# A softmax guard as a reduction with a constant column, the first half's sums of x moved into attention, and one clamp moved to ScalarE

## The chip, the cores and the metric

The kernel runs on one core of a Trainium2 chip. The metric is the device time of one execution in microseconds, taken as the median of several runs. The engines are named as in the profile: PE is TensorE (matmuls; PEld its weight loads), DVE is VectorE, ACT is ScalarE, POOL is GpSimd, and SP is the engine whose queue issues the DMAs.

## The reference

Three layers follow each other. The shapes are batch 2, 8 heads, sequence 576, head size 64, so 1152 tokens with 512 features; the mixture has 4 experts of width 1024, the last layer has width 1536. Everything is float32.

```python
# attention with a decay from the clamped, cumulated gates s
cum = np.cumsum(np.maximum(s, 0.0), axis=-1)
bias = -(cum[:, :, :, None] - cum[:, :, None, :])
scores = np.where(causal, -1e9, scale * q @ k.T + np.minimum(bias, 0.0))
attn = np.exp(scores - scores.max(-1, keepdims=True))
attn = attn / (attn.sum(-1, keepdims=True) + 1e-09)
x = attn @ v                                   # 1152 x 512
# a dense mixture of 4 experts
p = domain_probs / (domain_probs.sum(-1, keepdims=True) + 1e-09)
x = sum(p[:, e:e+1] * (np.maximum(x @ w1[e], 0.0) @ w2[e]) for e in range(4))
# a gated layer
g = x @ w_gate
out = (g / (1 + np.exp(-g)) * (x @ w_val)) @ w_out
```

## The kernel before

**Precision.** Dense products are made from three matmuls in a reduced format: each operand is held as a high part and a low part (`xh`, `xl` for x, `wah`, `wal` for an input weight, `woh`, `wol` for an output weight, `hh`, `hl` for the hidden layer), and high times high, high times low and low times high are added up in PSUM. Making a high part is a cast (helper `move`, L325 on ACT, L327 on DVE, L329 on POOL), making a low part is a subtraction (helper `minus`, L338, on DVE or POOL).

**Attention.** The sequence is cut into an early part (positions 0 to 255) and a late part (256 to 575). There are 16 pairs of heads: eight early ones and then eight late ones. For each pair PE makes the scores (`sp`, L528 to L547); DVE adds bias and mask and takes the row's minimum of the negated scores (`least`, L562, written to a small statistics tile `st`); ACT takes the exponential and its row sum (L571, to columns 8 to 11 of `st`); DVE adds 1e-9 to two row sums at a time and takes the reciprocal (`guard`, L577 and L578, 40 times in all); ACT or POOL scales the rows (`norm`, L333 or L335); PE transposes them (`tp`, L622); ACT or DVE copies the result (`p`, L325 or L327); PE multiplies with v (`po`, L681); ACT or DVE and then DVE write `xh` and `xl` (L697). The late part's decay comes from a scan over the clamped gates: `positive` (L394), `scan` (L397), `center` (L402, tile `sums`), a small store to memory (`rows`), from which each late pair's bias is loaded by DMA (`dql`, `d`; the latter gets a mask added, L493).

**Dense work.** Hidden units go in slices of 256 (a slice is an input weight and an output weight of 512 KB each). As soon as the first early x is done, input products (L1016 to L1018) and output products (L1177 to L1179) for the first 256 or 512 tokens are put between the attention steps on PE. Until the end of attention POOL alone makes the high and low parts of the weights (L329, L338). Each output product is scaled by its expert's share and added to an accumulator on DVE (`acc_a`, `acc_b`, L1275).

**The sums of x.** After attention, input products are made in a form with seven instead of eight block products (`seven`, L1116 to L1118). For it four sums of quarters of x are needed for the first 512 tokens and again for the other 640 (`sums_of_x`). One call makes, for two column blocks each, nine additions or subtractions into a temporary `tt` (18 instructions, L1055), eight casts (L325) and eight low parts (L338), that is 34 instructions of 128 x 256 elements for the first 512 tokens and of 128 x 320 for the rest. Before the change both calls stand behind the end of attention, when their tiles `xh0`, `xl0`, `xh512`, `xl512` are made; additions and low parts go to DVE or POOL, casts to ACT or DVE.

**What sets the order.** Nothing is scheduled at run time. A planner in the file (`Plan`) holds all tasks with estimated costs, their dependences, the buffers they take and a rank. It emits again and again the task that can start first by its own clock of each engine, and among equals the one of lowest rank. `any_of` lets it choose the engine too. What it emits is each engine's instruction order, so an instruction that has to wait holds up everything behind it on its engine. The planner has a clock of its own for the port that it takes DVE and POOL to share, but `guard` and `positive` do not count on it.

Of the kernel before, what the change touches and what calls it, by code (L numbers as in the profile page):

```python
# [1 line left out]

# [6 lines left out]
F32 = mybir.dt.float32  # L9
F32R = mybir.dt.float32r  # L10
I32 = mybir.dt.int32
U32 = mybir.dt.uint32
AF = mybir.ActivationFunctionType
ALU = mybir.AluOpType
# [89 lines left out]
def act(c, n=1):  # L104
    return n * 0.05 + 0.00084 * c
# [173 lines left out]
def attention_moe_swiglu(ctx, tc, q_early, q_late, k, v, s, dp, w1, w2, wg, wv, wo, out):  # L279
# [37 lines left out]
    def ring(name, n=2):  # L317
        return rings.setdefault(name, Ring(n))

    def any_of(engines, kind, c, run, deps, n=1, **kw):  # L320
        return add(choices(engines, kind, c, n), None, run, deps, port="vp" if kind in ("two", "copy", "scale") else "p", **kw)
# [27 lines left out]
    def attention(ap, ps):  # L349
# [43 lines left out]
        def positive(e, x):  # L393
            {"v": nc.vector, "p": nc.gpsimd}[e].tensor_scalar(sr[:, x], sr[:, x], 0.0, -1.0 / SC, op0=ALU.max, op1=ALU.mult)  # L394
# [15 lines left out]
            sb, ncum[:, early], ncum[:, P - 1:P], 1.0, op0=ALU.subtract, op1=ALU.mult), [t_scan], rank=-98)]  # L410
        for j in range(2):
            t_early.append(add("dve", 0.41, lambda j=j: rest(j), t_early[-1:], rank=-98))
        t = any_of("v", "fill", S - 2 * P, lambda e: positive(e, later), [t_sr2], rank=CUM2)
        t.at = CUMAT
        t_scan2 = add("dve", 0.95, lambda: scan(later), [t, t_scan], rank=CUM2)

# [6 lines left out]
        if FILLER:  # L423
            def begin():
                plan.filler = keep_on
                plan.clock["pe"] = 1.65
            t_id.note = begin

        raw, t_raw, loaded = {}, {}, {}

# [76 lines left out]
        def group(i, pi, ch, qbs):  # L507
# [42 lines left out]
            def least(x, lane, at, w):  # L550
                def run():
                    if "st" not in box:
                        box["st"] = ap.tile([P, 20], F32, name="st", tag="st", bufs=6)
                    if lane not in box["ns"]:
                        box["ns"][lane] = ap.tile([P, S], F32, name="ns", tag="ns", bufs=NS)
                    st, ns = box["st"][:, 2 * x:2 * x + 2], box["ns"][lane]
                    if two:
                        todo = [(s0, s1, y[:, :s1 - s0], decay[pi, 2][:, s0:s1]) for y, (s0, s1) in zip(box["sp"], spans)]
                    else:
                        todo = [(at, at + w, box["sp"][lane][:, at:at + w], mask[:, 2 * P - w:] if pi < EXACT else decay[pi][:, lane, :w])]  # L560
                    for y, (s0, s1, sp, bias) in enumerate(todo):
                        nc.vector.tensor_tensor_reduce(  # L562
                            ns[:, s0:s1], sp, bias, SC, st[:, 0:1] if y else 3.0e38, op0=ALU.add, op1=ALU.min, accum_out=st[:, y:y + 1])
                return run
# [9 lines left out]
            def guard(x, n):  # L574
                def run():
                    st = box["st"]
                    nc.vector.tensor_scalar(st[:, 12 + x:12 + x + n], st[:, 8 + x:8 + x + n], 1.0e-9, None, op0=ALU.add)  # L577
                    nc.vector.reciprocal(st[:, 16 + x:16 + x + n], st[:, 12 + x:12 + x + n])  # L578
                return run

            def norm(x, lane, at, w):
# [373 lines left out]
    def make_weights(need):  # L955

        stop = min(len(queue), queue.index(need) + AHEAD)
        while made["n"] < stop:
            queue[made["n"]].make(WRANK + made["n"])
            made["n"] += 1  # L960
# [68 lines left out]
            return make  # L1029
        return [item(c0) for c0 in range(0, NC, step)]  # L1030

    def sums_of_x(t0):

        n = (N - HALF if t0 else HALF) // 2
        box = late["T", t0]

        deps = needs_x(t0, t0 + 2 * n) + late.get("sums", [])
        done = box["done"] = {}

        def quarter(x, i, j, c):  # L1040
            return f32(x[:, 2 * i + c, t0 + j * n:t0 + j * n + n])
        tmp = {}
        rg = ring("tt")

        rank = WRANK + made["n"] - (0 if t0 else 2)
        SUB, ADD = ALU.subtract, ALU.add

        def total(name, x, y, op, deps, new=False):

            def task(c, at):  # L1050
                def run(on):
                    if new and c == 0:
                        tmp[name] = late["t"].tile([P, 6 * P], F32, name="tt", tag="tt", bufs=2)[:, :2 * n].rearrange("p (c n) -> p c n", c=2)
                    x_, y_ = (tmp[z][:, c] if isinstance(z, str) else quarter(*z, c) for z in (x, y))
                    {"v": nc.vector, "p": nc.gpsimd}[on].tensor_tensor(tmp[name][:, c], x_, y_, op=op)  # L1055
                return any_of(TADD, "two", n, run, at, take=[rg] if new and c == 0 else [], rank=rank)
            first = task(0, deps[0])
            return [first, task(1, deps[1] + ([first] if new else []))]

        def chain(*lists):  # L1060
            return [[x[c] for x in lists] for c in range(2)]

        def parts(i, name, t):
            done[i] = []
            for c in range(2):
                def high(on, c=c):
                    move(on, box["h"][:, i, c], tmp[name][:, c])

                def low(on, c=c):
                    minus(on, box["l"][:, i, c], tmp[name][:, c], box["h"][:, i, c])  # L1070
                hi = any_of(THIGH, "copy", n, high, [t[c]], rank=rank)
                done[i].append(any_of(TLOW, "two", n, low, [hi], rank=rank))
            return done[i]
        a1 = total("T1", (xh, 0, 1), (xh, 0, 0), SUB, [deps, deps], True)
        t = total("T1", "T1", (xl, 0, 1), ADD, chain(a1))
        t1 = total("T1", "T1", (xl, 0, 0), SUB, chain(t))
        a2 = total("T2", (xh, 1, 1), "T1", SUB, chain(t1), True)
        t2 = total("T2", "T2", (xl, 1, 1), ADD, chain(a2))
        u2 = parts(1, "T2", t2)
        u1 = parts(0, "T1", t1)  # L1080

        t = total("T1", "T2", (xh, 0, 0), SUB, chain(u1, t2))
        t3 = total("T1", "T1", (xl, 0, 0), SUB, chain(t))
        u3 = parts(2, "T1", t3)
        add(None, 0.0, None, u3, give=[(a1[0], rg)])
        t = total("T2", (xh, 1, 0), "T2", SUB, chain(u2, t3))
        u4 = parts(3, "T2", total("T2", "T2", (xl, 1, 0), ADD, chain(t)))
        add(None, 0.0, None, u4, give=[(a2[0], rg)])
        late["sums"] = [x for y in done.values() for x in y]
# [418 lines left out]
    def gates(ap):  # L1508
        dps = ap.tile([P, NT, E], F32, name="dps", bufs=1)
        got = [add("dma", (ISSUE, 0.06), lambda: nc.sync.dma_start(dps, dp), rank=GRANK)]  # L1510
        got[0].at = GATES

        def run():
            sm = const.tile([P, NT], F32, name="sm")
            nc.vector.reduce_sum(sm, dps, axis=AX.X)
            nc.vector.tensor_scalar(sm, sm, 1.0e-9, None, op0=ALU.add)
            nc.vector.reciprocal(sm, sm)
            nc.vector.tensor_tensor(pr, dps, sm.unsqueeze(2).to_broadcast([P, NT, E]), op=ALU.mult)
        return add("dve", 0.8, run, got, rank=10)
# [11 lines left out]
    with ExitStack() as st:  # L1531
        ps = st.enter_context(tc.tile_pool(name="psa", bufs=1, space=PSUM))
        late["hA"] = ctx.enter_context(tc.tile_pool(name="hA", bufs=2))
        ap = st.enter_context(tc.tile_pool(name="ap", bufs=2))
        for _ in attention(ap, ps):
            pass
        late["gates"] = gates(ap)
        make_weights(queue[0])
        while any(x.end is None for g in done_x for x in done_x[g]):
            if all(x.end is not None for x in done_x[0]):  # L1540
                feed()
            assert plan.step()
        while plan.step(lambda t: not getattr(t, "dense", False) and t.rank < 1000 and t.eng != "dma"):
            pass
    with ExitStack() as st:
        late["ps"] = st.enter_context(tc.tile_pool(name="psb", bufs=1, space=PSUM, reuse_waits="tile"))
        late["t"] = st.enter_context(tc.tile_pool(name="tm", bufs=2, reuse_waits="tile"))
        late["h"] = late["t"]
        late["acc"] = late["t"].tile([P, NT - HALF // P, DM], F32, name="acc_b", bufs=1)
        for t0, n in ((0, HALF), (HALF, N - HALF)):  # L1550
            late["T", t0] = {x: late["t"].tile([P, 4, 2, n // 2], F32R, name=f"x{x}{t0}", bufs=1) for x in "hl"}
            sums_of_x(t0)
        late["made_n"] = 0
        plan.held, plan.ported = HELD2, False
        rings["h"].n, rings["o"].n = 5, 3
        feed()
        while plan.step():
            feed()
# [70 lines left out]
```

## Time and profile before

| | us |
|---|---|
| median of 3 runs (lowest, highest) | 710.91 (709.16, 711.38) |
| profiled execution, device time | 710.5 |
| its span in the profile | 708.7 |
| attention: first instruction to last `xl` (L697) | about 0 to 126.7 |
| both calls of the sums of x (L1055, L338) | 127.7 to 163 |
| dense work alone, in the seven-product form where it can be | from there to 705 |

The profile counts an engine as busy from an instruction's start to its end. PE's matmuls are pipelined, so overlapping ones hide short gaps; the rows for PE that carry an idle time in brackets are stretches in which nothing was in flight. The engine's own rows then say what released it.

### The profile page before, as it was taken

To read this page: it belongs to the slowest core of one execution; us is meant where nothing else is said; L and a number is where in the kernel's file an instruction comes from. 1 tells how busy PE (TensorE), PEld (TensorE's weight loads), DVE (VectorE), ACT (ScalarE), POOL (GpSimd) and SP (SyncE) were. 2 spreads that over 40 slices of the span, in tenths; PEclk is the share of its full clock that TensorE was granted. 3 is DMA by queue.
4 is the path that set the end of the run, shared out by engine and by line. 5 is a ranking of instruction groups with operands and counts; after the bars stand their busy time and mean duration, and the time that the engine had idled before them with its cause. 6 is when DMAs were issued, how large, how long until landed. Compare 5 with 4: busy or idle time off the path is not lost.

```text
span 708.7 us, 11847 instructions
## 1 busy us (share of the span) xinstructions
PE 695.1 (98%) x4243; PEld 605.8 (85%) x4243; DVE 552.8 (78%) x1087; ACT 357.4 (50%) x760; POOL 455.5 (64%) x434
## 2 busy tenths in 40 slices
PE   8899999999999999999999999999999999999997
PEld 7676666777999899989988889998989999999996
DVE  7876656793488898999899998786876878777665
ACT  7688776335354646456546665456554323333110
POOL 2873333978545865667558677698998848484311
PEclk9999999999999999999999999999999999999999
DMA  6695650220242434435525555213012201000003
GB/s 197 207 316 174 193 155 1 60 90 31 90 149 93 175 120 162 152 120 191 194 90 192 194 179 178 74 41 105 6 60 83 68 30 61 31 31 1 1 1 133
DMA packets 30187, 78.45 MB, mean 111 GB/s; under 512 B 3488, under 2 KB 8096, under 8 KB 30128
## 3 DMA queue, kind: packets, MB, share of 16 engines
q1 hardware_dynamic: 29984, 77.56, 33.4%
q8 instruction: 33, 0.54, 0.3%
q14 instruction: 26, 0.21, 0.1%
q10 hardware_dynamic: 144, 0.13, 0.1%
HBM read 65.85 MB, written 11.83 MB: 110 GB/s over the span
## 4 chain that ended last, share of the span: by engine, by line
PE 87%; DVE 7%; ACT 2%; POOL 1%; issue 1%; DMA 0%; DVEq 0%; POOLq 0%; ACTq 0%
PE h L1116 12%; PE o L1177 12%; PE h L1118 12%; PE h L1117 12%; PE o L1178 12%; PE o L1179 12%; PE tp L622 3%; PE po L681 2%; DVE tt L1055 2%; PE sp L540 2%; PE h L1016 2%; PE h L1017 1%; PE h L1018 1%; ACT ns L571 1%; PE sp L528 1%
## 5 line engine op out<-in xcount | busy, mean ns | idle before, releaser
L1135 DVE TENSOR_TENSOR cc<-cc,h 128x320 f32<-128x320 f32 (+1 forms) x282 | 126.4, 454 | 53.6 <-PE h L1118 45.7
L1177 PE MATMUL o<-woh,hh 128*128 128x512 f32 x397 | 157.4, 397 | 2.6 <-DVE acc_a L1275 2.5
L1178 PE MATMUL o<-wol,hh 128*128 128x512 f32 x397 | 156.0, 393 | 0.0
L1179 PE MATMUL o<-woh,hl 128*128 128x512 f32 x397 | 155.0, 390 | 1.0 <-DVE hl L338 1.0
L338 POOL TENSOR_TENSOR wal<-raw,wah 128x512 fp32r<-128x512 f32 (+1 forms) x58 | 73.1, 1270 | 31.5 <-ACT wah L325 30.2
L1116 PE MATMUL h<-xh,wsh 128*128 128x320 f32 (+1 forms) x312 | 93.1, 298 | 0.1
L1118 PE MATMUL h<-xh,wsl 128*128 128x320 f32 (+1 forms) x312 | 92.8, 298 | 0.0
L1117 PE MATMUL h<-xl,wsh 128*128 128x320 f32 (+1 forms) x312 | 92.7, 297 | 0.0
L1179 PEld LDWEIGHTS o<-woh,hl 128*128 128x128 f32 x397 | 74.7, 188 | 17.9 <-DVE hl L338 1.4
L338 POOL TENSOR_TENSOR hl<-cc,hh 128x512 fp32r<-128x512 f32 (+1 forms) x29 | 43.6, 1504 | 70.0 <-ACT hh L1247 68.8
L1177 PEld LDWEIGHTS o<-woh,hh 128*128 128x128 f32 x397 | 74.7, 188 | 16.1 <-DVE acc_a L1275 3.4
L1178 PEld LDWEIGHTS o<-wol,hh 128*128 128x128 f32 x397 | 74.7, 188 | 10.7
L338 POOL TENSOR_TENSOR wol<-raw,woh 128x512 fp32r<-128x512 f32 x54 | 77.8, 1457 | 7.0 <-ACT woh L325 6.0
L1244 ACT ACTIVATE cc<-cc 128x640 f32<-128x640 f32 (+1 forms) x46 | 32.1, 697 | 88.8 <-DVE cc L1135 88.8
L1116 PE MATMUL h<-xh,wah 128*128 128x320 f32 (+1 forms) x234 | 69.7, 298 | 0.9 <-DVE cc L1135 0.9
L1118 PE MATMUL h<-xh,wal 128*128 128x320 f32 (+1 forms) x234 | 69.4, 297 | 0.0
L1117 PE MATMUL h<-xl,wah 128*128 128x320 f32 (+1 forms) x234 | 69.3, 296 | 0.0
L338 POOL TENSOR_TENSOR wsl<-sf,wsh 128x512 fp32r<-128x512 f32 x44 | 64.1, 1478 | 2.2 <-ACT wsh L325 2.2
L1275 DVE SCALAR_TENSOR_TENSOR acc_b<-o,pr,acc_b 128x512 f32<-128x512 f32 x75 | 55.5, 744 | 7.0 <-PE o L1179 6.8
L1116 PEld LDWEIGHTS h<-xh,wsh 128*128 128x128 f32 x312 | 58.9, 189 | 1.9 <-ACT cc L325 0.3
L1117 PEld LDWEIGHTS h<-xl,wsh 128*128 128x128 f32 x312 | 59.0, 189 | 1.4
L1118 PEld LDWEIGHTS h<-xh,wsl 128*128 128x128 f32 x312 | 59.0, 189 | 0.0
(149 smaller groups left out, 1644.7 us busy)
## 6 DMA issues: line engine op xcount, KB each, us to landing
raw<-in_w SPq DMA_DIRECT2D x42, 512.0 KB, 5.0
n<-hl SPq DMA_DIRECT2D x36, 256.0 KB, 2.3
raw<-n SPq DMA_DIRECT2D x18, 512.0 KB, 3.3
hh<-in_wg SPq DMA_DIRECT2D x12, 512.0 KB, 4.1
hh<-in_wv SPq DMA_DIRECT2D x12, 512.0 KB, 4.3
hh<-in_wo SPq DMA_DIRECT2D x12, 512.0 KB, 4.1
dql<-rows SPq DMA_DIRECT2D x8, 512.0 KB, 5.1
vr<-in_v SPq DMA_DIRECT2D x4, 640.0 KB, 3.9
```

The lines of the kernel that those rows point to most:

```text
L338: {"v": nc.vector, "p": nc.gpsimd}[e].tensor_tensor(to, x, f32(y), op=ALU.subtract)
L540: nc.tensor.matmul(sp[j][:, at:at + w], Q[half[j], x], K[half[j], :w], start=True, stop=False)
L622: nc.tensor.transpose(tp[:kn, x * P:x * P + P], box["ns"][lane][:, at + c * P:at + c * P + kn], ident)
L1116: nc.tensor.matmul(hp, wh, h, start=c == 0, stop=False)
L1117: nc.tensor.matmul(hp, wh, l, start=False, stop=False)
L1118: nc.tensor.matmul(hp, wl, h, start=False, stop=c == 1)
L1135: nc.vector.tensor_tensor(part(k), part(x), banks[i], op=ALU.add)
L1177: nc.tensor.matmul(op, hh[:, f, ts], wh[:, f, y], start=f == 0, stop=False, skip_group_check=check)
L1178: nc.tensor.matmul(op, hh[:, f, ts], wl[:, f, y], start=False, stop=False, skip_group_check=check)
L1179: nc.tensor.matmul(op, hl[:, f, ts], wh[:, f, y], start=False, stop=f == NF - 1, skip_group_check=check)
L1244: nc.scalar.activation(src()[:, o], src()[:, o], AF.Relu)
L1275: nc.vector.scalar_tensor_tensor(acc(t), bank_(), sc, acc(t), op0=ALU.mult, op1=ALU.add)
```

## The change

1. `guard`: instead of adding 1e-9 with `tensor_scalar`, DVE sums pairs with `reduce_sum`; the second member of each pair is a column of `st` that holds 1e-9 all the time. For this the six statistics tiles are made once, used in turn, and their columns 12 to 15 are filled by six small POOL memsets at the start.
2. The sums of x of the first 512 tokens are planned during attention, with their own tiles: additions and low parts on POOL alone, casts on ACT or DVE as before. Their rank (150) lies behind that of attention's own tasks and of the weights that are then due. The sums of the other 640 tokens stay where they were.
3. The later gates' positive part (128 x 320) is an ACT Relu with a scale, instead of a DVE `tensor_scalar` with max and multiply.

```diff
-        t = any_of("v", "fill", S - 2 * P, lambda e: positive(e, later), [t_sr2], rank=CUM2)
+        t = add("act", act(S - 2 * P) + 0.15, lambda: nc.scalar.activation(sr[:, later], sr[:, later], AF.Relu, scale=-1.0 / SC), [t_sr2], rank=CUM2)
...
+        stat = [ap.tile([P, 24], F32, name=f"st{i}", bufs=1) for i in range(6)]
+        stats = cycle(stat)
+        for x in stat:
+            add("pool", 0.1, lambda x=x: nc.gpsimd.memset(x[:, 12:16], 1.0e-9), [t_up], rank=-97)
...
-                        box["st"] = ap.tile([P, 20], F32, name="st", tag="st", bufs=6)
+                        box["st"] = next(stats)
...
-                    nc.vector.tensor_scalar(st[:, 12 + x:12 + x + n], st[:, 8 + x:8 + x + n], 1.0e-9, None, op0=ALU.add)
-                    nc.vector.reciprocal(st[:, 16 + x:16 + x + n], st[:, 12 + x:12 + x + n])
+                    nc.vector.reduce_sum(st[:, 20 + x:20 + x + n], st[:, 8:16].rearrange("p (y x) -> p x y", y=2)[:, x:x + n], axis=AX.X)
+                    nc.vector.reciprocal(st[:, 16 + x:16 + x + n], st[:, 20 + x:20 + x + n])
...
-    def sums_of_x(t0):
+    def sums_of_x(t0, pool=None, add_on=TADD, low_on=TLOW):
...
-        rg = ring("tt")
-        rank = WRANK + made["n"] - (0 if t0 else 2)
+        rg = ring("te" if pool else "tt")
+        rank = WRANK + (50 if pool else made["n"])
...
         late["gates"] = gates(ap)
+        late["T", 0] = {x: const.tile([P, 4, 2, HALF // 2], F32R, name=f"x{x}0") for x in "hl"}
+        sums_of_x(0, ap, "p", "p")
         make_weights(queue[0])
...
-        for t0, n in ((0, HALF), (HALF, N - HALF)):
-            late["T", t0] = {x: late["t"].tile([P, 4, 2, n // 2], F32R, name=f"x{x}{t0}", bufs=1) for x in "hl"}
-            sums_of_x(t0)
+        late["T", HALF] = {x: late["t"].tile([P, 4, 2, (N - HALF) // 2], F32R, name=f"x{x}{HALF}", bufs=1) for x in "hl"}
+        sums_of_x(HALF)
```

## Rows read from the trace of the kernel before

**Rows 1.** The page: busy time by engine, and the chain that ended last.
```profile
PE 695.1 (98%) x4243; PEld 605.8 (85%) x4243; DVE 552.8 (78%) x1087; ACT 357.4 (50%) x760; POOL 455.5 (64%) x434
...
PE 87%; DVE 7%; ACT 2%; POOL 1%; issue 1%; DMA 0%; DVEq 0%; POOLq 0%; ACTq 0%
```

**Rows 2.** Order of time, PE: start, duration, line, idle before, releaser.
```profile
24.43 0.87 PE L681 MATMUL po<-p,vr 128*64 128x256 f32 x8 [1.28 <-DVE xl L697]
25.99 0.70 PE L533 MATMUL sp<-k,qe 64*128 64x128 f32 x5 [0.28 <-DVE st L562]
28.78 1.09 PE L622 MATMUL tp<-ident,ns 128*128 128x128 f32 x3 [1.17 <-ACT ns L333]
...
146.99 0.50 PE L1177 MATMUL o<-woh,hh 128*128 128x512 f32 x1 [1.68 <-DVE acc_a L1275]
160.69 0.50 PE L1177 MATMUL o<-woh,hh 128*128 128x512 f32 x1 [0.87 <-DVE acc_a L1275]
```

**Rows 3.** Stretches: busy PE, PEld, DVE, ACT, POOL, granted clock, DMA share, GB/s.
```profile
28.00:29.00 1.00, 0.22 (x1) 0.18 (x1) 0.96 (x6) 0.67 (x2) 0.92 (x3) 0.75 0.98 364
29.00:30.00 1.00, 1.00 (x5) 0.82 (x5) 0.95 (x5) 1.00 (x6) 1.00 (x2) 0.50 0.97 300
...
31.00:32.00 1.00, 1.00 (x7) 1.00 (x6) 0.40 (x4) 0.36 (x1) 1.00 (x2) 0.55 0.72 135
```

**Rows 4.** Order of time, DVE, 20 to 30 us.
```profile
20.91 1.39 DVE L394 TENSOR_SCALAR sr<-sr 128x320 f32<-128x320 f32 x1
22.34 0.98 DVE L397 TENSOR_TENSOR_SCAN ncum<-one,ncum,sr 128x320 f32<-128x320 f32 x1
...
23.96 0.41 DVE L697 TENSOR_TENSOR xl<-po,xh 128x256 fp32r<-128x256 f32 x1
26.80 1.24 DVE L577 TENSOR_SCALAR st<-st 128x2 f32<-128x2 f32 x1 [0.87 <-ACT ns L571]
29.49 0.18 DVE L1515 TENSOR_REDUCE sm<-dps 128x9 f32<-128x36 f32 x1
```

**Rows 5.** Order of time, POOL, 20 to 30 us.
```profile
20.85 1.27 POOL L338 TENSOR_TENSOR wal<-raw,wah 128x512 fp32r<-128x512 f32 x1
...
26.74 1.27 POOL L338 TENSOR_TENSOR wol<-raw,woh 128x512 fp32r<-128x512 f32 x1
...
28.68 1.27 POOL L338 TENSOR_TENSOR wol<-raw,woh 128x512 fp32r<-128x512 f32 x1
```

**Rows 6.** The guard's two lines: ns min/median/max, first and last start.
```profile
L577 DVE TENSOR_SCALAR st<-st x40: 142/169/1236, 7.7 to 119.7; 128x2 f32<-128x2 f32 x32, 128x1 f32<-128x1 f32 x8
...
L578 DVE RECIPROCAL st<-st x40: 162/166/167, 7.9 to 119.9; 128x2 f32<-128x2 f32 x32, 128x1 f32<-128x1 f32 x8
```

**Rows 7.** The tile `tt`: ns min/median/max, first and last start.
```profile
L325 ACT CAST xh<-tt x36: 299/407/462, 130.3 to 506.7; 128x256 fp32r<-128x256 f32 x24, 128x320 fp32r<-128x320 f32 x8, 128x128 fp32r<-128x128 f32 x4
...
L1055 DVE TENSOR_TENSOR tt<-tt,xl x12: 409/773/1509, 128.6 to 160.6; 128x320 f32<-128x320 f32 x7, 128x256 f32<-128x256 f32 x5
```

**Rows 8.** Stretches, columns as in rows 3.
```profile
45.00:95.00 50.00, 49.70 (x353) 34.14 (x354) 33.49 (x114) 41.05 (x102) 22.27 (x29) 1.00 0.64 202
```

**Rows 9.** Order of time, DVE, at 45 and 52 us.
```profile
44.97 0.40 DVE L697 TENSOR_TENSOR xl<-po,xh 128x256 fp32r<-128x256 f32 x1
...
52.49 0.23 DVE L493 TENSOR_TENSOR d<-d,tri 128x64 f32<-128x64 f32 x1 [1.42 <-DMA d<-rows]
```

**Rows 10.** Groups, whole span: line, shapes, count, busy us, mean ns, idle before.
```profile
L1055 POOL TENSOR_TENSOR tt<-xh 128x256 f32<-128x256 f32 x2 | 1.4, 744 | 0.0
...
L1613 POOL MEMSET const-float32-1.0<- 128x1 f32 x1 | 0.1, 98 | 0.0
```

**Rows 11.** The scaling on POOL (L335) alone: length, busy, clock, DMA share, GB/s.
```profile
45.00:95.00 50.00, 5.21 (x8) 1.00 0.64 202
```

**Rows 12.** Order of time, DVE, 144 to 147 us.
```profile
144.29 1.98 DVE L1055 TENSOR_TENSOR tt<-xh 128x320 f32<-128x320 f32 x2
146.20 0.74 DVE L1275 SCALAR_TENSOR_TENSOR acc_a<-o,pr,acc_a 128x512 f32<-128x512 f32 x1
```

More of the change, by code (lines that the diff above doesn't have):

```diff
@@ L1 @@
 from contextlib import ExitStack
+from itertools import cycle
 import concourse.bass as bass
@@ L1052, in run @@
                     if new and c == 0:
-                        tmp[name] = late["t"].tile([P, 6 * P], F32, name="tt", tag="tt", bufs=2)[:, :2 * n].rearrange("p (c n) -> p c n", c=2)
+                        tmp[name] = (pool.tile([P, 2 * n], F32, name="te", tag="te", bufs=2) if pool else late["t"].tile(
+                            [P, 6 * P], F32, name="tt", tag="tt", bufs=2)[:, :2 * n]).rearrange("p (c n) -> p c n", c=2)
                     x_, y_ = (tmp[z][:, c] if isinstance(z, str) else quarter(*z, c) for z in (x, y))
                     {"v": nc.vector, "p": nc.gpsimd}[on].tensor_tensor(tmp[name][:, c], x_, y_, op=op)
-                return any_of(TADD, "two", n, run, at, take=[rg] if new and c == 0 else [], rank=rank)
+                return any_of(add_on, "two", n, run, at, take=[rg] if new and c == 0 else [], rank=rank)
             first = task(0, deps[0])
@@ L1071, in parts @@
                 hi = any_of(THIGH, "copy", n, high, [t[c]], rank=rank)
-                done[i].append(any_of(TLOW, "two", n, low, [hi], rank=rank))
+                done[i].append(any_of(low_on, "two", n, low, [hi], rank=rank))
             return done[i]
```

## The prediction

> **What bounds the kernel now.** I read the page first. PE is busy for 98% of the span and makes 87% of the chain that ended last [rows 1]: the time is PE's work plus the stretches in which PE stands still or runs at a lower clock. So I looked for PE's own waits, in order of time. Up to 180 us, apart from the start and short ones, there are two clusters [rows 2]. At 24 to 29 us PE stands for 1.28, 0.28 and 1.17 us, together 2.73 us, released by `xl`, by the statistics and by the scaling. At 147 and 161 us it stands for 1.68 and 0.87 us, together 2.55 us, both times for a DVE accumulation into `acc_a`. The stretches of one microsecond then show a cost behind the first cluster: the granted clock is 0.75 at 28 us, 0.50 from 29 us (the 1.2 GHz level instead of 2.4) and 0.55 at 31 us, after PE was busy for only 0.22 us of the one at 28 [rows 3]. At half clock three microseconds do about 1.55 us of work, so about 1.45 us more is lost there (0.50 + 0.50 + 0.45, the middle second being like the one before it). First cluster: 2.73 + 1.45 = 4.18 us.
>
> DVE's order tells why the first cluster stands. The later gates' clamp L394 takes 1.39 us [rows 4] and ends where a POOL subtraction that ran beside it ends (20.85 + 1.27 = 22.12, the clamp at 22.30) [rows 5]. The scan follows, 0.98 us, then the centring up to 23.96, and only then the `xl` for which PE waits [rows 4]. The guard at 26.80 takes 1.24 us [rows 4], and ends at 28.04, just behind a POOL subtraction that ends at 28.01 [rows 5]; it is what the scaling, and so PE's third wait, waited for. Over the kernel a guard's first half takes 142 to 1236 ns with a median of 169, while the reciprocal right behind it always takes 162 to 167 [rows 6]. So this instruction waits for POOL, and the reciprocal doesn't.
>
> **The change, part by part.**
>
> *Guard.* The reduction reads four elements per row and writes two. The nearest row is the reduction over 128x36 at 29.49 us: 0.18 us, although it ran within a POOL subtraction (28.68 to 29.95) [rows 4, 5]. I take 0.17 us, as for an unhindered guard; bounds 0.14 and 0.18, which over 40 guards is -1.2 to +0.4 us of DVE time, none of it on PE's path unless PE waits. The guard's excess over 0.17 us goes: 1.07 us at 26.80.
>
> The Trainium skill ("VectorE: DVE Perf Modes", section "Rules for kernel authors") warns that a `tensor_reduce` on the hot path is the slowest DVE operation and should be restructured. The trace does not bear that out at this size (0.18 us beside POOL [rows 4]). By that rule the guards would get dearer; by the row they lose their wait.
>
> *Clamp.* 1.39 us leave DVE. On ACT the nearest row is a cast of 128x320 or less from SBUF, at most 462 ns [rows 7]; I take 0.46 us, bounds 0.30 (the least of that row) and 0.92 (with one more such cast ahead of it). ACT is not PE's releaser around 20 us. If it comes late, the scan stands on DVE, and behind it the `xl` that PE waits for; then up to the whole 1.28 us stays.
>
> *Gain in the first cluster.* With 1.39 us off DVE ahead of `xl`, PE's 1.28 us wait just goes; with the guard at 0.17 the 1.17 us wait shrinks to about 0.1; without these PE has no reason to fall to the lower clock. The ceiling is 4.18 us, the floor 0 (another engine is late by as much). What is next late: the transfers. From 45 to 95 us they fill 0.64 of the DMA engines [rows 8], and at 52 us DVE stood 1.42 us for a bias transfer, whose request follows PE's progress [rows 9]. I take 3.2 us: the ceiling less 1.0 us.
>
> *Sums of the first 512 tokens.* 26 instructions go to POOL: 18 additions and 8 low parts at 744 ns [rows 10], 19.3 us. Eight casts of about 0.41 us, 3.3 us, mostly on ACT [rows 7]. They can begin when the last early pair's `xl` is done, at 45.4 us (44.97 + 0.40) [rows 9]. The cover: from 45 to 95 us POOL is busy for 22.3 of 50 us [rows 8], so it has 27.7 us free, more than 19.3. ACT is busy for 41.1 of 50 us [rows 8]; with 3.3 us it comes to 44.4, 89%. If the cover is gone, each of the eight POOL scalings in that stretch [rows 11] can be held up by at most one addition, 0.74 us. Half of that for eight is 3.0 us; with dense products in front of most of them I put a fifth of it, 0.6 us, on PE; bounds 0 and 5.9.
>
> The Trainium skill ("GPSIMD Engine Reference", section "Engine selection") says two-input elementwise work belongs on VectorE and is about twice as slow on GpSimd. The trace agrees on the ratio (744 ns against 409 alone on DVE [rows 7, 10]). By that rule the move is a loss, 8.7 us of engine time (26 x 0.335); by the stretches POOL's time there is idle. It stands behind the third rival.
>
> *Behind attention.* Half of the 68 instructions leave the stretch of 127 to 163 us. That is not worth 2.55 us by itself: PE did not stand while the first 512 tokens' sums ran (127.7 to 144 us). Both waits lie in the second half's sums: at 144.29 two of its subtractions take 1.98 us on DVE, and the accumulation that PE needs stands behind them [rows 12]. These stay, and still take 409 to 1509 ns each [rows 7], but they start some 16 us sooner and with no backlog on DVE. Floor 0, ceiling 2.55; I take half, 1.3 us.
>
> *Six memsets*: 98 ns each [rows 10], 0.6 us of POOL before the first guard at 7.7 us [rows 6]. POOL's first use for attention is later, so nothing. Uncovered it would cost 0.6 us.
>
> The new tasks also make the planner emit another order. I can't price that without building; up to about 1 us either way is my guess and lies inside the bounds.
>
> **The sum.** Against the profiled execution of 710.5 us (span 708.7, the rest lies outside): 710.5 - 3.2 - 1.3 + 0.6 = 706.6. The median is 0.4 us above that execution: **707.0 us**. No change from faster or slower is told within 0.3%, 2.1 us.
>
> **Rivals.**
>
> 1. *The gain is taken back.* The first waits go, but PE then runs ahead of transfers and ACT (0.64 and 82% busy [rows 8]) and stands later in attention; the second half's sums stall PE as before. For it: the wait on a bias transfer [rows 9]. Against: from 45 to 95 us PE hardly stands [rows 8]. Left over is about 1 us: 709.9.
> 2. *Everything goes.* The first cluster gives its whole 4.18, the second its 2.55, and POOL's work stays hidden: 710.9 - 6.7 = 704.2. For it: the guard's waits elsewhere also go (up to 1.24 us for one [rows 6]). Against: DVE and POOL still share the second half's sums.
> 3. *Slower: POOL's sums hold up the scaling.* An addition that has just begun is not broken off; a scaling that comes ready behind it waits up to 0.74 us, and so does the transpose that stands in PE's fixed order. ACT can hardly take the eight over: at POOL's 0.65 us each (5.21 / 8 [rows 11]) they would bring its 44.4 to 49.6 of 50 us. With the whole 0.74 on each of the eight: +5.9, less the 3.2 of the first cluster, so +2.7: 713.6. It decides once the dense products that PE has between a guard and its transpose last less than the delay in more than four of the eight (3.2 / 0.74 = 4.3). Against: in that stretch PE is in flight for 49.7 of 50 us [rows 8].
> 4. *The guard still waits*, since the change does not do what it says: the reduction stands for POOL like the addition. Then POOL's busier queue makes it worse, and only the clamp's 1.3 us and the second cluster remain: 709 to 712. The reduction's row speaks against it [rows 4]; I count it with 1 and 3.
>
> **How the numbers follow.** My forecast, 704.9 to 708.7, gets 0.50; rival 2 0.15; rival 1, with the milder form of 4, 0.21; rival 3, with the worse form of 4, 0.14. So faster 0.65, same 0.21, slower 0.14. The range runs from 703.5 (below it a twentieth, part of rival 2) to 711.6 (above it most of rival 3).
>
> **What would show it.** The guard's first half at 0.14 to 0.19 us in all 40 cases; no DVE clamp at 21 us and `xl` about 1.4 us sooner; a clock of 1.00 from 28 to 32 us; 26 POOL instructions of the sums between 42 and 120 us; fewer or shorter waits for `acc_a` between 126 and 150 us. Wrong would make it: waits of PE for scaling or ACT between 40 and 120 us, a DVE scan that waits for ACT, or the second half's sums stalling PE for 2.5 us again.

## The result, and the profile after

The changed kernel takes 703.79 us (median of 4 runs, 702.54 to 705.42), the one before 711.08 beside it (4 runs, 709.16 to 711.38). The ratio is 0.9904, 95% interval [0.9877, 0.9932]. That is 3.2 us below my forecast and inside its range. The profiled execution took 702.54 us, its span is 700.7: it is the fastest of the four, 1.2 us below their median.

The page of the changed kernel, answering to [rows 1]:

```profile
PE 690.0 (98%) x4240; PEld 600.8 (86%) x4240; DVE 539.8 (77%) x1080; ACT 356.2 (51%) x751; POOL 463.4 (66%) x456
...
PE 89%; ACT 4%; DVE 4%; DMA 2%; issue 1%; SPq 0%; DVEq 0%; ACTq 0%
```

PE remains the bound. DVE's share of the chain that ended last fell from 7% to 4%. PE's waits of 0.33 us and more between 20 and 180 us, in order of time (start, duration, line, idle before, releaser), answering to [rows 2]:

```profile
30.12 0.44 PE L628 MATMUL tp<-ident,ns 128*128 128x128 f32 x2 [0.54 <-ACT ns L334]
...
54.99 0.66 PE L628 MATMUL tp<-ident,ns 128*128 128x128 f32 x4 [0.72 <-ACT ns L334]
...
74.58 0.66 PE L628 MATMUL tp<-ident,ns 128*128 128x128 f32 x4 [0.39 <-ACT ns L334]
...
141.65 0.50 PE L1184 MATMUL o<-woh,hh 128*128 128x512 f32 x1 [0.33 <-DVE acc_a L1282]
```

The 2.73 us of waits at 24 to 29 us are gone, the 2.55 us for `acc_a` are 0.33. Three waits for ACT's scaling have come instead, 0.54 + 0.72 + 0.39 = 1.65 us. The granted clock answers to [rows 3] (busy PE, clock, DMA share, GB/s):

```profile
28.00:29.00 1.00, 1.00 (x11) 1.00 0.31 95
29.00:30.00 1.00, 0.58 (x4) 1.00 0.71 226
...
31.00:32.00 1.00, 1.00 (x14) 1.00 1.03 379
```

Now the guard's lines, answering to [rows 6] (ns min/median/max, first and last start), and then DVE's own order from 20 to 30 us, answering to [rows 4]:

```profile
L583 DVE TENSOR_REDUCE st<-st x40: 140/157/159, 7.4 to 118.1; 128x2 f32<-128x4 f32 x32, 128x1 f32<-128x2 f32 x8
...
L584 DVE RECIPROCAL st<-st x40: 163/166/167, 7.6 to 118.3; 128x2 f32<-128x2 f32 x32, 128x1 f32<-128x1 f32 x8
```

```profile
21.10 1.22 DVE L398 TENSOR_TENSOR_SCAN ncum<-one,ncum,sr 128x320 f32<-128x320 f32 x1
22.35 0.56 DVE L403 TENSOR_SCALAR sums<-ncum 128x576 f32<-128x576 f32 x1
22.83 0.41 DVE L703 TENSOR_TENSOR xl<-po,xh 128x256 fp32r<-128x256 f32 x1
...
26.27 1.14 DVE L1523 TENSOR_SCALAR sm<-sm 128x9 f32<-128x9 f32 x1
```

The new guard shows a wait for POOL in none of 40 cases (159 ns at most, against 1236). The wait hasn't left DVE, though: the scan takes 1.22 us instead of 0.98, and a small `tensor_scalar` on another tile 1.14 us; both run beside POOL. `xl` comes 1.13 us sooner than before (22.83 against 23.96).

The moved sums, by their tile `te`, and the stretch that [rows 8] shows (busy PE, PEld, DVE, ACT, POOL, clock, DMA share, GB/s):

```profile
L1062 POOL TENSOR_TENSOR te<-te,xl x10: 722/738/749, 51.0 to 78.4; 128x256 f32<-128x256 f32 x10
L339 POOL TENSOR_TENSOR xl<-te,xh x8: 721/728/791, 55.1 to 80.7; 128x256 fp32r<-128x256 f32 x8
```

```profile
45.00:95.00 50.00, 48.89 (x338) 33.06 (x338) 32.13 (x112) 40.76 (x103) 39.62 (x53) 1.00 0.58 188
```

POOL's 26 instructions run from 45.7 to 81.4 us, at 721 to 791 ns. POOL is busy for 39.6 of 50 us there (22.3 before), and PE has no wait of 0.33 us or more for a scaling of POOL's in this profile.

### The profile page after: what moved, and what is told of

Same layout as the page of the kernel before. It is cut to its first block, busy times and chain, and to the rows that moved or that the text cites. A ratio compares the mean times of both kernels' runs of the same rounds, so it can differ in the third digit from the quotient of the medians.

```text
span 700.7 us, 11844 instructions
## 1 busy us (share of the span) xinstructions
PE 690.0 (98%) x4240; PEld 600.8 (86%) x4240; DVE 539.8 (77%) x1080; ACT 356.2 (51%) x751; POOL 463.4 (66%) x456
## 4 chain that ended last, share of the span: by engine, by line
PE 89%; ACT 4%; DVE 4%; DMA 2%; issue 1%; SPq 0%; DVEq 0%; ACTq 0%
PE o L1184 13%; PE o L1185 12%; PE o L1186 12%; PE h L1123 12%; PE h L1124 12%; PE h L1125 12%; PE po L687 3%; PE tp L628 2%; PE h L1022 2%; PE h L1024 2%; PE h L1023 2%; ACT ns L577 2%; PE sp L546 2%; DVE tt L1062 1%; PE sp L534 1%; DMA d<-rows 1%
```

## The experiments

The kernel before ran beside them in three sets: medians 710.93 (29 runs), 711.08 (17) and 710.79 (11). Where runs of different sets are set against each other, I take its median over the first two, 710.98 (46 runs). "Milestones" are the first and the last start of the product `h<-xh,wsh` in the seven-product form: what lies ahead of the first is attention and its surroundings, what lies between the two is the dense stretch. The milestones are those of one profiled execution, which can lie up to 2 us off its version's median (sums alone: 704.43 against 706.36).

| | us, median (lowest to highest, runs) | ratio [95%] | milestones of its profile, difference |
|---|---|---|---|
| before, 1st profile | | | 188.6, 691.3: 502.7 |
| guard alone | 709.40 (708.13 to 711.04, 12) | 0.9987 [0.9975, 0.9998] | 188.7, 691.8: 503.1 |
| clamp alone | 709.30 (708.59 to 710.23, 11) | 0.9984 [0.9974, 0.9994] | 187.4, 690.1: 502.7 |
| guard and clamp | 708.34 (706.57 to 712.17, 12) | 0.9977 [0.9962, 0.9992] | 185.6, 688.7: 503.1 |
| tiles' place alone | 708.95 (707.33 to 710.86, 12) | 0.9976 [0.9966, 0.9985] | 187.0, 688.1: 501.1 |
| sums moved alone | 706.36 (704.43 to 706.58, 5) | 0.9942 [0.9925, 0.9959] | 184.1, 685.2: 501.1 |
| sums and clamp | 705.66 (704.96 to 706.18, 5) | 0.9928 [0.9915, 0.9942] | 184.9, 686.0: 501.1 |
| sums and guard | 703.85 (703.57 to 704.37, 4) | 0.9905 [0.9890, 0.9919] | 183.3, 684.4: 501.1 |
| all (the change) | 703.79 (702.54 to 705.42, 4) | 0.9904 [0.9877, 0.9932] | 182.2, 683.3: 501.1 |
| all, sums on DVE or POOL | 706.23 (704.97 to 707.17, 6) | 0.9938 [0.9917, 0.9958] | 185.9, 687.6: 501.7 |

**The parts alone.** First the guard and the clamp, each alone and together, without the moved sums. The main line of the guard's edit (the six tiles, their memsets and the reciprocal's operand change with it), then the clamp's:

```diff
-                    nc.vector.tensor_scalar(st[:, 12 + x:12 + x + n], st[:, 8 + x:8 + x + n], 1.0e-9, None, op0=ALU.add)
+                    nc.vector.reduce_sum(st[:, 20 + x:20 + x + n], st[:, 8:16].rearrange("p (y x) -> p x y", y=2)[:, x:x + n], axis=AX.X)
```

```diff
-        t = any_of("v", "fill", S - 2 * P, lambda e: positive(e, later), [t_sr2], rank=CUM2)
+        t = add("act", act(S - 2 * P) + 0.15, lambda: nc.scalar.activation(sr[:, later], sr[:, later], AF.Relu, scale=-1.0 / SC), [t_sr2], rank=CUM2)
```

> The reduction with the constant column alone; the clamp stays on DVE and both calls of the sums stay behind attention. PE's order is the same as before, instruction by instruction, so only waits can change. Theory A (DVE instructions that wait for POOL cost PE its waits at 24 to 29 us): the guard's first half lies at 0.14 to 0.19 us in all 40 cases, PE's wait of 1.17 us at 28.8 us goes, the one of 1.28 us at 24.4 us (clamp) stays; the clock may still fall. Gain 1.5 to 2.5 us, about 709.0 us. Rival B (the other order of the instructions made the gain): under 0.5 us, 710.6 us or more.

> The clamp on ACT alone; guard by addition, both calls of the sums behind attention. Theory A: PE's wait of 1.28 us at 24.4 us goes, the one of 1.17 us for a guard stays and the clock still falls after it: gain 1 to 2 us, about 709.5 us. Rival B: this edit makes the planner emit another order from about 20 us on, and that gives most of the gain: 3 us or more, 708 us or less. A third reading: the guards meet POOL's subtractions by chance of timing, so new waits of a guard take the place of the old ones and the time stays at 711.

> Guard and clamp as in the changed kernel, both calls of the sums behind attention. Theory A: the first cluster goes with its clock (4.2 us) and the two waits for the accumulation stay at about 2.5 us: gain 3.5 to 4.5 us, about 707 us. Rival B: PE's order differs from before in a dozen places near 20 to 30 us only, so little more than guard alone: 709 us.

Measured: 709.40, 709.30 and 708.34 us. Both together are worth 2.6 us by the medians (710.98 - 708.34) and 1.6 by the ratio, not 3.2. For the guard alone theory A has the size by the medians (1.6 us, 0.9 by the ratio) but not the waits: the one for `xl` shrinks too, from 1.28 to 0.20 us. For the clamp alone theory A has the size (1.7 us by the medians, 1.1 by the ratio) and the lost wait for `xl`, while the clock stays at 1.00 from 20 to 40 us and two guards at 24 and 27 us wait in other places (0.99 and 1.28 us). For both together neither theory's time came (about 707 and 709 us): the first cluster goes and the 2.5 us for `acc_a` stay, as theory A has it, but part is given back. With the guard alone, DVE at 20 to 24 us shows why the clamp's wait is no simple sum:

```profile
20.69 0.32 DVE L395 TENSOR_SCALAR sr<-sr 128x320 f32<-128x320 f32 x1
21.05 1.77 DVE L398 TENSOR_TENSOR_SCAN ncum<-one,ncum,sr 128x320 f32<-128x320 f32 x1
22.86 0.56 DVE L403 TENSOR_SCALAR sums<-ncum 128x576 f32<-128x576 f32 x1
23.34 0.40 DVE L703 TENSOR_TENSOR xl<-po,xh 128x256 fp32r<-128x256 f32 x1
```

Here the clamp stays on DVE and takes 0.32 us: it comes just ahead of POOL's subtraction. Now the scan behind it waits instead, 1.77 us against 0.98. Clamp and scan take 2.1 us here and 2.4 us in [rows 4]. What the first cluster gives is then lost again further on. In the profile of the guard alone (711.04 us, the slowest of its twelve) PE has two later waits, and the clock is at 0.66 from 38 to 40 us, so that the dense stretch begins at 188.7 us, no sooner than before. With both parts PE waits 1.72 us for a scaling on POOL. The guard alone, then both parts:

```profile
36.53 1.17 PE L546 MATMUL sp<-k,ql 64*128 64x512 f32 x3 [1.12 <-DVE st L568]
...
96.24 0.66 PE L628 MATMUL tp<-ident,ns 128*128 128x128 f32 x4 [1.00 <-POOL ns L336]
```

```profile
52.70 1.09 PE L628 MATMUL tp<-ident,ns 128*128 128x128 f32 x8 [1.72 <-POOL ns L336]
```

**The sums moved, alone.**

```diff
+        late["T", 0] = {x: const.tile([P, 4, 2, HALF // 2], F32R, name=f"x{x}0") for x in "hl"}
+        sums_of_x(0, ap, "p", "p")
...
-        for t0, n in ((0, HALF), (HALF, N - HALF)):
-            late["T", t0] = {x: late["t"].tile([P, 4, 2, n // 2], F32R, name=f"x{x}{t0}", bufs=1) for x in "hl"}
-            sums_of_x(t0)
+        late["T", HALF] = {x: late["t"].tile([P, 4, 2, (N - HALF) // 2], F32R, name=f"x{x}{HALF}", bufs=1) for x in "hl"}
+        sums_of_x(HALF)
```

> The first 512 tokens' sums of x during attention on POOL alone; guard by addition and clamp on DVE as before. Theory A: PE's two waits for the accumulation shrink from 2.55 us to about 0.3 us (gain 2.2 us), but the guards meet a busier POOL between 40 and 95 us: their first half's total rises from 11.6 us to 16 us or more, and part of that reaches PE: gain 0.5 to 2 us, 709 to 710.5 us. Rival B: gain 3 us or more. Rival C (POOL's sums hold up the scaling): slower than before, 712 us or more.

Measured: 706.36 us, ratio 0.9942, so 4.1 us by the ratio and 4.6 by the medians: rival B. Most of the change's gain lies in the part that I had priced at 0.7 us net. Theory A's price for it did not come either: the 40 old guards take 10.0 us in all, not 16, and less than the 11.6 us of the kernel before. Its waits for `acc_a` (engine, line, waited for; us in total, times, longest):

```profile
PE o L1179 <- DVE acc_a L1277: 0.4, 1, 0.4
```

That is 2.5 us in [rows 2], so about 2.2 us are explained. The milestones show another piece: the dense stretch between them is 1.6 us shorter (501.1 against 502.7) in every version with the sums moved to POOL, though no wait of PE there is gone.

**The place of the tiles.** In the dense stretch the 256-column products differ, and nothing else by as much: 912 of them from 200 to 680 us take 281.6 ns each before and 279.9 after. What is moved with the sums is also where their results lie: the two tiles that these products stream in. So one version moves the tiles' place alone; the sums run on the same engines, and the order on each engine is that of before.

```diff
+        late["T", 0] = {x: const.tile([P, 4, 2, HALF // 2], F32R, name=f"x{x}0") for x in "hl"}
         make_weights(queue[0])
...
         for t0, n in ((0, HALF), (HALF, N - HALF)):
-            late["T", t0] = {x: late["t"].tile([P, 4, 2, n // 2], F32R, name=f"x{x}{t0}", bufs=1) for x in "hl"}
+            if t0:
+                late["T", t0] = {x: late["t"].tile([P, 4, 2, n // 2], F32R, name=f"x{x}{t0}", bufs=1) for x in "hl"}
             sums_of_x(t0)
```

> Before, with one thing of the change: the two tiles with the first 512 tokens' sums lie in the pool that is open for the whole kernel, not in the late one; the sums themselves run where and when they ran before. From 200 to 680 us the 256-column products into h take 281.6 ns each in the four versions profiled so far without the moved sums or with the other two parts alone (before, guard, clamp, both), and 279.9 ns in the two with the moved sums; 912 x 1.7 ns = 1.6 us. Theory (the tiles' place does it): 279.9 ns here, the two acc_a waits stay at about 2.5 us, and the time is 710.9 - 1.6 = 709.3. Rival (the order of the moved work does it): 281.6 ns and 710.9, ratio within 0.999 and 1.001.

Measured: 708.95 us, ratio 0.9976, so 1.7 us by the ratio and 2.0 by the medians; dense stretch 501.1 us. The products of 256 columns, by shape, from 200 to 680 us (busy us, mean ns, idle before); first before, then with the tiles' place changed:

```profile
L1118 PE MATMUL h<-xh,wsl 128*128 128x256 f32 x128 | 36.1, 282 | 0.0
...
L1118 PE MATMUL h<-xh,wal 128*128 128x256 f32 x96 | 26.9, 281 | 0.0
```

```profile
L1118 PE MATMUL h<-xh,wsl 128*128 128x256 f32 x128 | 35.8, 280 | 0.0
...
L1118 PE MATMUL h<-xh,wal 128*128 128x256 f32 x96 | 26.8, 279 | 0.0
```

And its wait for `acc_a`, which stays:

```profile
PE o L1177 <- DVE acc_a L1275: 2.5, 2, 1.7
```

The theory holds: the place alone gives the shorter products and leaves the waits for `acc_a`. (This profile, 707.33 us, is the fastest of twelve; it starts the dense stretch at 187.0 us for another reason, the first cluster, to which I come back below.) By the order of allocation, which no trace shows, the edit also shifts tiles that lie behind the new ones, the `wa` weights among them, but not the `ws` weights. The products with `ws` weights, of which three in four stream from the two tiles, shorten by 2.6 ns (107.5 against 108.5 us for 384); those with `wa`, of which one in three does, by 1.0 ns (80.5 against 80.8 us for 288). That points to the streamed operand and not to the weights. The 512-column products, which don't stream these tiles, also shorten a little, from 393.3 to 392.7 ns (some 940 of them), so other tiles' places may have a part. So the moved sums are two gains, 2.0 us for the place (1.6 of them seen in the dense stretch) and 2.6 us (708.95 - 706.36) for the earlier work. The profiles bear the second out: those of the tiles' place alone and of the sums alone run within 0.5 us of each other up to 45 us, and reach the dense stretch at 187.0 and 184.1 us, 2.9 us apart, 2.2 of them the waits that go.

Two tests of what in the place matters, one run each. The first swaps the two pairs of tiles in the late pool; the second shifts the changed kernel's tiles by 64 bytes.

```diff
-        for t0, n in ((0, HALF), (HALF, N - HALF)):
+        for t0, n in ((HALF, N - HALF), (0, HALF)):
             late["T", t0] = {x: late["t"].tile([P, 4, 2, n // 2], F32R, name=f"x{x}{t0}", bufs=1) for x in "hl"}
+        for t0 in (0, HALF):
             sums_of_x(t0)
```

> Before, with the two pairs of tiles for the sums allocated in the other order in the late pool: the second half's (320 columns) at byte 118,624 of each partition, where the first half's were, and the first half's (256 columns) at byte 139,104. Nothing else differs. Measured: 256-column products 281.6 ns with the tiles at 118,624 and 279.8 at 46,880; 320-column ones 309.4 at 135,008. Theory (the bytes from 118,624 on are the slower place): 256 columns 279.9 and 320 columns slower by 1 ns or more. Rival (the late pool is the slower place, or what is read beside it): 256 columns stay at 281.6, 320 at 309.4.

```diff
+        const.tile([P, 16], F32, name="pad0")
         late["T", 0] = {x: const.tile([P, 4, 2, HALF // 2], F32R, name=f"x{x}0") for x in "hl"}
```

> The changed kernel with 64 bytes of padding per partition ahead of the two tiles for the first 512 tokens' sums, so that they, and all that lies behind them, begin at 96 modulo 128 as in the kernel before, and not at 32. Theory (the place as a whole, not its low bits): 279.9 ns for a 256-column product, and the time of the changed kernel, 703.8 within 0.3%. Rival (the low bits): 281.6 ns, 705.4.

Measured: swapped, 710.72 us (one run); 256 columns 281.6 ns and 320 columns 309.2, as before. So it isn't those bytes (the positions are the allocator's; no trace shows an address), and my theory for this run falls. Shifted by 64 bytes, 703.86 us (one run) and a dense stretch of 501.1 us, as in the changed kernel; the 256-column products at 280.8 ns fit neither expectation, the 512-column ones are 0.9 ns shorter still (391.8). So the low bits move single products, but not the time of this run. What makes the place ahead of the other tiles better than two places in the late pool stays open.

**The change less one part.** First the old guard put back, then the old clamp.

```diff
-                    nc.vector.reduce_sum(st[:, 20 + x:20 + x + n], st[:, 8:16].rearrange("p (y x) -> p x y", y=2)[:, x:x + n], axis=AX.X)
+                    nc.vector.tensor_scalar(st[:, 12 + x:12 + x + n], st[:, 8 + x:8 + x + n], 1.0e-9, None, op0=ALU.add)
```

> The changed kernel with the old guard (a tensor_scalar addition of 1e-9, then the reciprocal). PE's order is that of the changed kernel. Theory (the parts add up): the guard is worth about 0.9 us as alone (710.9 against 709.4), so 703.8 + 0.9 = 704.7. With POOL busy for 8 to 9.8 of each 10 us from 40 to 80 us the old guard waits there too: its total over 40 guards above the 10.0 to 10.8 us of the other versions with it, but hidden behind dense products. Rival (with POOL so busy the old guard's waits reach PE): 706 or more, PE waits of 0.5 us and more behind scalings between 40 and 90 us.

```diff
-        t = add("act", act(S - 2 * P) + 0.15, lambda: nc.scalar.activation(sr[:, later], sr[:, later], AF.Relu, scale=-1.0 / SC), [t_sr2], rank=CUM2)
+        t = any_of("v", "fill", S - 2 * P, lambda e: positive(e, later), [t_sr2], rank=CUM2)
```

> The changed kernel with the old clamp on DVE or POOL by the planner's choice. Theory (the parts add up): the clamp on ACT is worth about 1.1 us as alone (710.9 less 709.3 is 1.6 by medians, 1.1 by the ratio), so 704.9 to 705.4. Rival (the clamp's wait for POOL only moves to the scan behind it, so ACT's clamp is worth nothing once the sums are moved): 703.8. In the stretch from 20 to 24 us the scan takes 1.0 us where the clamp waited and 1.8 us where it did not.

Measured: without the new guard 705.66 us, so the guard is worth 1.9 us by the medians, with intervals that overlap; with the old clamp it is 2.5 (706.36 to 703.85), and there they don't. Without the new clamp 703.85, as with it: on top of the other two parts the clamp on ACT is worth 0.1 us, which is nothing that can be told. The old guard's line, with the sums and the new clamp, then with the sums alone (whole kernel, busy us, mean ns, idle before):

```profile
L578 DVE TENSOR_SCALAR st<-st 128x2 f32<-128x2 f32 (+1 forms) x40 | 12.6, 314 | 13.1 <-ACT ns L572 12.8
...
L578 DVE TENSOR_SCALAR st<-st 128x2 f32<-128x2 f32 (+1 forms) x40 | 10.0, 249 | 15.7 <-ACT ns L572 15.6
```

The new form takes 6.1 to 6.2 us (40 x 154 ns). That the old one waits more where POOL is busier is not borne out: over the versions that have it, it takes 9.1 us (tiles' place alone) to 12.6, and 12.5 in the swapped version, whose sums stand behind attention. For the guard neither time came (704.7; 706 or more).

Where the guard's 1.9 to 2.5 us lie is not shown. The profiled execution of the sums alone is the fastest of its five and does not have the first cluster (PE stands there for 0.58 and 0.20 us); it reaches the dense stretch only 0.8 us behind that with the new guard (184.1 and 183.3), and PE's first transposes are already 1.6 us apart (10.16 and 8.53), before a guard has waited in either.

For the clamp the rival holds. Part of its gain is the scan's loss, and the planner puts two score passes (0.29 and 0.42 us) ahead of the scan where the clamp stood. DVE in the version with the sums and the new guard, but the old clamp:

```profile
20.29 0.32 DVE L395 TENSOR_SCALAR sr<-sr 128x320 f32<-128x320 f32 x1
20.64 1.78 DVE L398 TENSOR_TENSOR_SCAN ncum<-one,ncum,sr 128x320 f32<-128x320 f32 x1
...
22.93 0.40 DVE L703 TENSOR_TENSOR xl<-po,xh 128x256 fp32r<-128x256 f32 x1
```

`xl` starts at 22.93 here and at 22.83 with the clamp on ACT. The scan reads a tile of ones and the gates, POOL's subtraction two tiles as well. The Trainium skill ("SBUF — State Buffer", section "Who interferes with whom") says that a DVE instruction with two SBUF inputs contends with a GpSimd instruction that reads SBUF, and that `tensor_reduce` on trn2 never contends; the 1.77 to 1.78 us of the scan and the 140 to 159 ns of the reduction agree.

**Does each execution lose the first cluster?** The kernel before, unchanged, profiled a second time.

> The kernel before, unchanged, for a second profile of it. My prediction took the 4.18 us of the first cluster (2.73 us of waits at 24 to 29 us and 1.45 us of half clock) as what every execution loses. Theory (it depends on how POOL's subtractions fall against DVE's clamp and guards in that execution): waits and clock at 20 to 40 us differ from those of the first profile by 0.5 us or more in the sum, the time by as much. Rival (every execution loses the same): 1.3 + 0.3 + 1.2 us of waits and a clock of 0.5 for three microseconds again.

Measured: 710.37 us (one run). The second profile has the waits of the first, 0.3 us earlier, as the rival has it:

```profile
24.13 0.87 PE L681 MATMUL po<-p,vr 128*64 128x256 f32 x8 [1.28 <-DVE xl L697]
...
28.49 1.04 PE L622 MATMUL tp<-ident,ns 128*128 128x128 f32 x3 [1.17 <-ACT ns L333]
```

But two other profiles speak for the theory. The version with the tiles' place alone has the order of the kernel before on every engine, with its guard and clamp, and its profile does not have this cluster. (Nor has that of the sums alone, whose order is the same up to 45 us.) PE's first transposes start 1.5 us later in it. Before, then the tiles' place alone:

```profile
9.15 0.90 PE L622 MATMUL tp<-ident,ns 128*128 128x128 f32 x6
```

```profile
10.62 0.96 PE L622 MATMUL tp<-ident,ns 128*128 128x128 f32 x6
...
23.95 0.44 PE L622 MATMUL tp<-ident,ns 128*128 128x128 f32 x2 [0.56 <-POOL ns L335]
24.59 1.23 PE L681 MATMUL po<-p,vr 128*64 128x256 f32 x8 [0.20 <-DVE xl L697]
```

So DVE meets POOL otherwise: the clamp starts at 21.43 us, ahead of POOL's subtraction at 21.67, and not behind it as before (20.91 and 20.85). It takes 0.33 us instead of 1.39, and the guard behind it 0.20 instead of 1.24:

```profile
21.43 0.33 DVE L394 TENSOR_SCALAR sr<-sr 128x320 f32<-128x320 f32 x1
21.80 1.82 DVE L397 TENSOR_TENSOR_SCAN ncum<-one,ncum,sr 128x320 f32<-128x320 f32 x1
...
26.31 0.20 DVE L577 TENSOR_SCALAR st<-st 128x2 f32<-128x2 f32 x1 [0.87 <-ACT ns L571]
```

The 2.73 us are thus what an execution loses whose DVE comes a few tenths of a microsecond late against POOL's subtraction, not a fixed cost. Why the first ten microseconds differ, I did not find out.

The clock is another matter. The swapped version has the order of the kernel before too, and all three waits of the first cluster, and the clock stays at 1.00 behind them (busy PE, clock, DMA share, GB/s):

```profile
28.00:29.00 1.00, 0.23 (x1) 1.00 1.00 377
29.00:30.00 1.00, 0.93 (x8) 1.00 1.01 307
```

It still reaches the dense stretch at 188.5 us, against 188.6 with the drop: at 33 us it is 1.2 us ahead, at 40 us 0.2, with a wait of 0.47 us for ACT between. Of the 57 runs of the kernel before in the three sets, 30 have a mean granted clock of 0.994 to 0.997 and a median of 711.22 us, 27 have 0.999 or 1.0 and a median of 710.21. I read this as the drop to the 1.2 GHz level in about half of the executions; the two halves lie 1.0 us apart. The profiled one, with its drop, has 0.997, and 25 of the 30 lie lower, so these lose more clock than it does. All 4 runs of the changed kernel have 1.0. Over the versions of the table, 0.997 or less comes in 35 of 74 runs with both the old guard and the old clamp, and in 2 of 54 with either part new: so the drop does go with them, as I had forecast.

**The moved sums on either engine.** The change binds additions and low parts to POOL. Here the planner is free to use DVE.

```diff
-        sums_of_x(0, ap, "p", "p")
+        sums_of_x(0, ap)
```

> The changed kernel, with the first 512 tokens' sums still during attention, but free to go to VectorE or GpSimd by the planner's choice (the change binds their 18 additions and 8 low parts to GpSimd). Theory (POOL's time there is idle and DVE has some too, so either engine will do): 703.8 within 0.3%. Rival (on DVE they stand ahead of the guards and the score passes, and beside POOL they contend): PE waits behind the statistics between 45 and 90 us, 705.5 or more. Other rival (a faster engine ends them sooner): below 703.

Measured: 706.23 us, 2.4 us worse than the change by the medians, though the two intervals overlap a little. DVE takes 15 of the 26. At 53 us, in order of time, DVE, then ACT, then PE:

```profile
53.82 1.89 DVE L1062 TENSOR_TENSOR te<-te,xl 128x256 f32<-128x256 f32 x2
55.62 0.74 DVE L1280 TENSOR_SCALAR acc_a<-o,pr 128x512 f32<-128x512 f32 x1
56.28 0.14 DVE L583 TENSOR_REDUCE st<-st 128x2 f32<-128x4 f32 x1
```

```profile
56.72 1.33 ACT L334 ACTIVATE ns<-ns,st 128x512 f32<-128x512 f32 x2 [0.58 <-DVE st L584]
```

```profile
57.50 0.66 PE L628 MATMUL tp<-ident,ns 128*128 128x128 f32 x4 [1.41 <-ACT ns L334]
```

Two additions stand ahead of a guard; the scaling and the transpose behind it come late, and PE stands for 1.41 us. The Trainium skill ("GPSIMD Engine Reference", section "Engine selection") sends elementwise additions to VectorE; here leaving them free to go there costs 2.4 us. DVE feeds PE in this stretch; the planner's order changes with the choice too, and how much of the 2.4 us that makes is not shown.

## Why the prediction was right on the whole and wrong in its terms

By medians, one way from 710.98 to 703.79 us goes: tiles' place 2.0, sums earlier 2.6, guard 2.5, clamp 0.1; in another order the parts would come out otherwise (guard and clamp without the sums: 2.6 together). My sum had 3.2 for the first cluster, 1.3 behind attention and -0.6 for the sums' side cost, 3.9 in all before the step to the median. The tiles' place, which I did not see, took the time from some 705.8 to 0.3 us above the lower end of my range. That the rest comes near in the sum, 5.2 against 3.9 us, is in part luck: hardly a term has its size for the reason that I gave.

- *First cluster, 3.2 us*: 2.6 (sums moved alone, 706.36, against all, 703.79). The guard's step held (0.14 to 0.18 forecast, 0.140 to 0.159 measured), and by the medians the guard brings nearly all of this, wherever it lies. The step "with 1.39 us off DVE ahead of `xl`" gave 1.13 us for `xl`, but is worth nothing of its own (0.1 us): with the new guard DVE reaches the old clamp soon enough that it takes 0.32 us, and the scan waits instead. The ceiling of 4.18 us was read from one execution: the same order has the waits in three profiles and not in the fourth, and by the mean clocks only about half of the executions have the drop. The profile with the waits and without the drop gained 0.1 us by it up to the dense stretch, not 1.45. And part is taken back, as rival 1 has it: 1.65 us of waits for ACT's scaling in the profile after.
- *Behind attention, 1.3 us*: 2.2 us of waits go. The step was right (the second half's sums start sooner) and I had halved its size without need. Their first subtraction starts at 121.39 us on POOL, not at 144.29 [rows 12], 23 us sooner where I said 16. The slowest are as slow as before (1.58 us for one on DVE in either profile), but PE's wait for an accumulation is down to 0.33 us.
- *Sums on POOL, 0.6 us loss*: none seen. Rival 3 fell: PE has no such wait for a scaling on POOL in the profile after (in the one with the 64 bytes there is one, of 0.30 us). ACT carries 40.8 of 50 us there, not the 44.4 that I added up.
- *No term at all for the tiles' place, 2.0 us.* I read `const.tile` for `late["t"].tile` as a matter of when the tile can be written. It is also an address, and over half of the 912 products of 256 columns stream from there.
- *Rival 2* named almost the measured time, 704.2, from other terms: 4.18 + 2.55. That is luck: the first of these is 2.6, and the tiles' place fills the difference.
- *Rival 4* fell with the guard's row.

## What to carry to other kernels

Where an instruction on one engine waits for another engine, look at what stands behind it before counting the wait as gained: the next instruction with the same need can inherit it, as the scan did here; the reduction, a form that showed no wait, was the part that paid. When a change moves a tile, separate its place from its timing with a version that moves the place alone. The engine that is slower for an operation can be the right one if the faster one feeds the bound. A wait that hangs on how two engines' instructions fall against each other can be absent in the next execution of the same order: a lone profile should be set beside others, and beside the spread of all runs, before its waits or a drop of the clock in it are priced in full.

## What the runs showed of the hardware that was not expected

- A product that streams 256 columns takes 281.6 or 279.8 ns (mean of 912, before and with the tiles' place alone) by where the two tiles lie, with the same order and weight loads of 188 to 189 ns in either. In two places of the late pool it is the longer, ahead of the other tiles the shorter. Products of 320 columns take 309.2 to 309.5 ns in all versions.
- A scan of 128x320 takes 0.98 us with POOL's subtraction out of the way and 1.77 to 1.82 us beside it; a `tensor_scalar` over 128x320 takes 1.39 us when it starts 0.06 us behind the subtraction, and 0.33 when it starts 0.24 us ahead. A `tensor_scalar` over 128x9 takes 1.14 us beside one, a reduction over four elements per row never over 160 ns in any version.
- The mean granted clock was 0.997 or less in 30 of 57 executions of one and the same program, and 0.999 or more in the other 27. Both of its profiles have the wait of 1.17 us and a granted clock of 0.50 right behind it; the swapped version's has the same wait and 1.00.
